# Attention, mixture of experts and a SoLU layer in one launch: row products at full array width, a two-step scale of v, and another order of the attention's steps

## The chip, the cores and the metric

The kernel runs on one NeuronCore of a Trainium2 chip. The engines are named as the profile names them: PE is TensorE (PEld its weight loads), DVE is VectorE, ACT is ScalarE, POOL is GpSimd, and SP is SyncE, which here only issues DMAs. The metric is the device time of one execution in microseconds (us), lower is better. Of the kernel before, three runs took 585.15, 590.14 and 594.05 us, median 590.14 us.

## The reference

Three stages follow one another. First, attention over 2 batches of 8 heads, 768 tokens, head size 64, where a query sees only the keys of its own cluster: each query and key goes to the nearest of 16 centroids, and only pairs with equal clusters count.

```python
q_assign = np.argmax(np.einsum('bhsd,hcd->bhsc', q_n, c_n), axis=-1)
k_assign = np.argmax(np.einsum('bhsd,hcd->bhsc', k_n, c_n), axis=-1)
mask = q_assign[:, :, :, None] == k_assign[:, :, None, :]
scores = scale * np.matmul(q, k.transpose(0, 1, 3, 2))
scores = np.where(mask, scores, -1000000000.0)
scores = scores - np.max(scores, axis=-1, keepdims=True)
attn = np.exp(scores)
attn = attn / (np.sum(attn, axis=-1, keepdims=True) + 1e-09)
return np.matmul(attn, v).astype(np.float32)
```

Its 1536 x 512 result goes through a mixture of 8 experts (each token to the expert of its largest logit: `relu(x @ w1[e]) @ w2[e]`, times two gates), and then through a dense layer: `h = x @ w_in`, SoLU (`h * softmax(h)`), layer norm with a gain, and `@ w_out`. All in single precision.

## The kernel before

The attention takes the 16 heads in eight pairs, `p` = 0 to 7; pairs 0 to 3 are batch 0. A pair's queries and keys stand transposed in one tile `w`, split in a high and a low part, so that products in the fast format keep single precision. Rows 64 to 79 of `w` hold one-hot clusters, which add a huge penalty to a score across clusters. A pair is made of these steps, each a short function that issues a few instructions on several engines:

- `hi`, `lo`, `moves`, `sims`, `red`, `arg0` to `arg2`, `aux0`, `aux1`: split queries and keys, move parts of `w` by DMA, compare with the centroids, take the nearest, and bring the one-hot rows into `w` (by PE, ACT and DMA). For pair 0 `mask` does the last of these straight from PSUM (line 434).
- `x` p.j (j = 0 to 11): one block of 128 queries by all 768 keys on PE (line 485, two matmuls into the one PSUM buffer `pm`), and DVE takes each row's largest (line 487, into column 16 of the tile `ohb` of the pair). The next `x` waits for that reduction, since there is one buffer. `y` does the same in two halves through the two score banks `pS` (lines 498 to 500).
- `row` p.h.half: turns three columns of largest scores into one row. Three matmuls (line 508) have one column of `ohb` as weights and the identity as moving operand, and write PSUM partition 64 (96 in pair 0); ACT negates the row into `w` (line 510).
- `vs0`, `vs1`, `vs2`: a power of two that scales v. DVE takes the largest of v in each partition (line 449); PE turns that column into a row (line 453), DVE takes its largest and makes the power of two on partition 0 (lines 455 to 458); PE sends it to all partitions by a matmul with ones (line 461), DVE copies it out (line 463). `vsp0`, `vsp1` split v by it (ACT line 474, DVE line 476).
- `S` p.u.part: scores of 128 keys by 384 queries (lines 540 and 541) into a bank `pS`, of which there are two, and ACT takes their exponential (line 550). `L` p.u.part: the low part of it, on DVE (`v`) or POOL (`p`), line 558. `A` p.u.part: 18 matmuls of probabilities by v (lines 574 to 576). After a head's last one DVE divides (lines 581 to 584).
- `tr`, `log`, `acc`: a pair's share of the expert logits. `g0.0` (lines 645 to 647), `g0.0.5` and others: place the tokens of batch 0 once pairs 0 to 3 are done. `warmN`: N matmuls on zeros.

Nothing schedules this at run time. Each engine executes its own instructions strictly in the order in which the program issued them, and waits on semaphores. That order is the string `FLAT`, some 800 names of such steps; a loop near the end calls them in turn. A second string, `MOE`, orders the experts' stage in the same manner.

Of the kernel before, what the change touches and what calls it, by code (L numbers as in the profile page):

```python
# [57 lines left out]
S1.4.0 x1.10 lo30p aux21 vs21 S1.4.1 S1.5.0 hi31 L1.1.0p A0.11.1 L1.2.0p x1.11 sims31 red31 tr00 A1.0.0 L1.4.0p S1.5.1
arg30 row111 S1.6.0 vs22 x2.0 S1.6.1 lo31v A1.1.0 tr01 L1.3.0p S1.7.0 S1.7.1 A1.2.0 log0 S1.8.0 arg31 x2.1 acc0 vsp20
A1.3.0 S1.8.1 L1.6.0p S1.9.0 y2.2 x2.3 A1.4.0 L1.8.0p S1.9.1 arg32 L1.5.0p row200 L1.7.0p ld4 S1.10.0 L1.9.0p x2.4  # L60
S1.10.1 aux30 y2.5 A1.5.0 moves3 S1.11.0 x2.6 row201 aux31 S1.11.1 A1.6.0 hi40 S2.0.0 vsp21 sims41 A1.7.0 L1.10.0p
S2.0.1 L1.11.0p late x2.7 zero3 zero4 S2.1.0 vs30 A1.8.0 S2.1.1 x2.8 y2.10 A1.9.0 red41 sims40 ld5 hi41 L2.0.0p x2.9
# [25 lines left out]
S7.5.0 x7.10 row710 A6.10.0 A6.11.0 L7.2.0p L7.3.0v S7.6.0 S7.7.0 x7.11 A7.0.0 A7.1.0 L7.4.0p L7.5.0v tr60 S7.8.0
S7.9.0 tr61 A7.2.0 L7.6.0p L7.7.0v S7.10.0 S7.11.0 log6 row711 A7.3.0 A7.4.0 L7.8.0p L7.9.0v S7.0.1 S7.1.1 acc6 pick0
A7.5.0 A7.6.0 L7.10.0p L7.11.0v pick1 S7.2.1 S7.3.1 pick2 A7.7.0 A7.8.0 L7.0.1p L7.1.1v S7.4.1 S7.5.1 A7.9.0 A7.10.0  # L90
L7.2.1p L7.3.1v S7.6.1 S7.7.1 A7.11.0 A7.0.1 L7.4.1p L7.5.1v w0 S7.8.1 S7.9.1 tr70 A7.1.1 A7.2.1 L7.6.1p L7.7.1v
S7.10.1 S7.11.1 log7 A7.3.1 A7.4.1 L7.8.1p L7.9.1v acc7 g1.0
# [1379 lines left out]
```

## Time and profile before

| | |
|---|---|
| runs | 585.15, 590.14, 594.05 us |
| profiled execution | 591.26 us |
| its span, first to last instruction | 589.5 us |
| mean granted TensorE clock | 0.986 |
| PE busy | 559.0 us, 95% |
| DVE busy | 407.8 us, 69% |
| ACT busy | 295.4 us, 50% |
| POOL busy | 259.0 us, 44% |

The attention lasts until about 256 us of the span, the experts until about 440 us, the dense layer to the end. PE stands beside its time in the whole span, DVE and POOL have most of theirs in the attention. A timeline row gives the start of a merged group in us from the span's start, its length, engine, source line, operation, output and input by the program's names, shapes and count; in brackets is how long the engine sat idle before, and whose end let it go. Lengths of matmuls include their latency, so the pace of PE is read from the starts.

### The profile page before, as it was taken

The page shows a single profiled execution, that of the slowest core. Times are in us where ns is not written, and L with a number is a line of the kernel's source. Part 1 is how long each engine was busy: PE and PEld are TensorE (multiplying, and loading weights), DVE is VectorE, ACT ScalarE, POOL GpSimd, SP SyncE. Part 2 cuts the span into 40 slices and gives each one's busy share as a digit, 9 for nine tenths or more (in the row PEclk, how much of TensorE's full clock was granted, in tenths as well). Part 3 has the DMA queues.
Part 4 walks back from the last instruction along what each step waited for, and adds up shares of the span by engine and source line. Part 5 has one row for each costly group of instructions (what it writes and reads, how often), then busy time and mean ns, then how long its engine had stood idle before and what let it go on. Part 6 is the DMA issues. An engine that isn't in the chain of part 4 may idle for free. (4 is left out here: it accounts for less than half of the span.)

```text
span 589.5 us, 12359 instructions
## 1 busy us (share of the span) xinstructions
PE 559.0 (95%) x4661; PEld 473.4 (80%) x4663; DVE 407.8 (69%) x814; ACT 295.4 (50%) x635; POOL 259.0 (44%) x285
## 2 busy tenths in 40 slices
PE   6999999999989999999999998999999999999995
PEld 2566678777768888898999998989997788888884
DVE  6788987778776889847667588887646845654550
ACT  5765766766745565423222467667655522332230
POOL 7467687888674777530000000320406742333221
PEclk9999999999986999999999999999999999999999
DMA  7258559547231111599939577683300000001000
GB/s 251 82 116 264 138 147 278 148 102 238 62 75 43 34 55 38 188 353 398 378 116 389 198 241 260 217 267 100 100 2 3 0 37 18 19 18 37 18 37 36
DMA packets 28866, 81.06 MB, mean 138 GB/s; under 512 B 5356, under 2 KB 5868, under 8 KB 28804
## 3 DMA queue, kind: packets, MB, share of 16 engines
q1 hardware_dynamic: 26020, 70.80, 37.8%
q0 software_dynamic: 2784, 9.44, 4.4%
q8 instruction: 38, 0.62, 0.4%
q14 instruction: 24, 0.20, 0.1%
HBM read 56.17 MB, written 11.53 MB: 115 GB/s over the span
## 5 line engine op out<-in xcount | busy, mean ns | idle before, releaser
L558 POOL TENSOR_TENSOR pl<-pe 128x768 f16<-128x768 f32 (+1 forms) x99 | 130.6, 1333 | 60.7 <-ACT pe L550 56.5
L550 ACT ACTIVATE pe<-pS 128x384 f32<-128x384 f32 x192 | 88.3, 489 | 68.9 <-PE pS L541 56.7
L487 DVE TENSOR_REDUCE ohb<-pm 128x1 bf16<-128x768 f32 x79 | 75.4, 954 | 31.1 <-PE pm L485 30.6
L540 PE MATMUL pS<-w 81*128 81x384 f32 (+1 forms) x192 | 77.9, 406 | 3.7 <-DVE mh L499 2.4
L541 PE MATMUL pS<-w 128*128 128x384 f32 x192 | 68.1, 355 | 0.0
L574 PE MATMUL pa<-v,pe 128*128 128x65 f16 x576 | 65.1, 197 | 0.0
L574 PEld LDWEIGHTS <-pe 128*128 128x128 bf16 x576 | 53.3, 99 | 14.0 <-issue 11.7
L575 PE MATMUL pa<-v,pe 128*128 128x64 f16 x576 | 64.3, 197 | 0.0
L576 PE MATMUL pa<-v,pl 128*128 128x65 f16 x576 | 64.0, 195 | 0.0
L575 PEld LDWEIGHTS <-pe 128*128 128x128 bf16 x576 | 54.4, 99 | 0.3
L576 PEld LDWEIGHTS <-pl 128*128 128x128 f16 x576 | 54.4, 100 | 0.0
L1034 POOL TENSOR_TENSOR wk<-rw,wk 128x512 fp32r<-128x512 f32 x13 | 18.0, 1395 | 73.9 <-ACT wk L1033 62.0
L485 PE MATMUL pm<-w 80*128 80x512 f32 (+1 forms) x158 | 45.7, 372 | 4.0 <-DVE ohb L487 2.9
L540 PEld LDWEIGHTS pS<-w 81*128 81x128 f32 (+1 forms) x192 | 38.3, 200 | 11.1 <-issue 3.2
L1335 ACT ACTIVATE e<-h,sm,smeta 128x512 f32<-128x512 f32 x24 | 18.5, 774 | 56.7 <-DVE sm L1331 56.7
L1330 DVE TENSOR_REDUCE sm<-h 128x1 f32<-128x512 f32 x24 | 15.4, 685 | 44.5 <-PE h L1041 41.5
L1033 ACT ACTIVATE wk<-rw 128x512 fp32r<-128x512 f32 x62 | 36.6, 631 | 10.4 <-DMA rw<-in_w_dram 8.0
L1034 DVE TENSOR_TENSOR wk<-rw,wk 128x512 fp32r<-128x512 f32 x49 | 34.7, 727 | 8.9 <-ACT wk L1033 8.5
L541 PEld LDWEIGHTS pS<-w 128*128 128x128 f32 x192 | 39.0, 203 | 0.1
L1039 PE MATMUL pf<-m,c 128*128 128x512 f32 x96 | 38.9, 405 | 0.0
L1039 PE MATMUL h<-m,x 128*128 128x512 f32 x96 | 37.7, 393 | 0.4 <-PEq L1295 0.4
L1040 PE MATMUL pf<-m,c 128*128 128x512 f32 x96 | 38.0, 395 | 0.0
(294 smaller groups left out, 1451.1 us busy)
## 6 DMA issues: line engine op xcount, KB each, us to landing
rw<-in_w_dram SPq DMA_DIRECT2D x31, 512.0 KB, 4.4
wk<-in_w_dram SPq DMA_DIRECT2D x25, 512.0 KB, 7.9
w<-w SPq DMA_DIRECT2D x42, 192.0 KB, 3.8
xs_d<-zrow SPq DMA_DIRECT2D x8, 512.0 KB, 5.1
w_w<-in_w_dram SPq DMA_DIRECT2D x8, 512.0 KB, 7.3
raw<-in_qT_dram SPq DMA_DIRECT2D x8, 384.0 KB, 3.7
raw<-in_kT_dram SPq DMA_DIRECT2D x8, 384.0 KB, 4.6
vraw<-in_v_dram SPq DMA_DIRECT2D x8, 384.0 KB, 5.7
```

Source lines behind the costliest of these rows:

```text
L485: nc.tensor.matmul(pm[:, c0:c1], w[0:80, M0 + h, 0, t * 128 : t * 128 + 128], w[0:80, M0 + h, 1, c0:c1], start=True, stop=True)
L487: nc.vector.tensor_reduce(out=s["oh"][:, t, 0, h, C : C + 1], in_=pm, op=ALU.max, axis=AX.X)
L540: nc.tensor.matmul(pS, w[0:kr, M0 + h, 1, ts], w[0:kr, M0 + h, 0, c0:c1], start=b0 == 0, stop=False, skip_group_check=True)
L541: nc.tensor.matmul(pS, w[:, B0 + h, 1, ts], w[:, B0 + h, 0, c0:c1], start=False, stop=True, skip_group_check=True)
L550: nc.scalar.activation(pe[:, e0 - b0 : e0 + n], s["bank"][:, : kb * n], AF.Exp, scale=0.125)
L558: eng.tensor_tensor(out=pl, in0=pe, in1=ph, op=ALU.subtract)
L574: nc.tensor.matmul(pa[:, o0 : o0 + D + 1], ph[:, qs], vh, start=(t == 0 and qt == q0), stop=False, skip_group_check=True)
L575: nc.tensor.matmul(pa[:, o0 : o0 + D], ph[:, qs], vl, start=False, stop=False, skip_group_check=True)
L576: nc.tensor.matmul(pa[:, o0 : o0 + D + 1], pl[:, qs], vh, start=False, stop=(t == NT - 1), skip_group_check=True)
L1034: (eng or nc.vector).tensor_tensor(out=t[:, 1, :], in0=rw, in1=t[:, 0, :].bitcast(F32), op=ALU.subtract)
L1039: nc.tensor.matmul(out, a[0], b[0], start=first, stop=False, skip_group_check=True)
L1040: nc.tensor.matmul(out, a[0], b[1], start=False, stop=False, skip_group_check=True)
```

## The change

Four things, none of which alters what is computed.

1. `row`: the one column of weights is read 65 times (97 in pair 0), so that the product fills PSUM partitions 0 to 64 and not 64 alone. ACT still reads the one row. In `order` this shows as an output of 65x128 where 1x128 stood. The count stays: 96 matmuls.
2. `mask` of pair 0: 80 columns of weights, into partitions 0 to 79, where 16 columns into partitions 64 to 79 stood (24 matmuls). The tile before `ohb0` is 64 columns longer, so that there is something to read.
3. `vs`: the column of largest values is read 128 times as weights against the identity, in single precision, so that every partition has the whole row; DVE reduces and makes the power of two on all 128 partitions. The second matmul, its copy on DVE and one PSUM tile of each pair fall away.
4. `FLAT`: up to `S3.11.0` the string is the old one without `vs02`, `vs12`, `vs22`, `vs32`. From there to the end of the attention, which is from about 136 us of the old span, steps stand in another order. `x5.4` and `x7.2` become `y`, `L4.9.0` and `L5.8.0` go from POOL to DVE, `L6.5.0` from DVE to POOL; in pair 7 four go from POOL to DVE and three from DVE to POOL; `warm1` and `warm4` in pair 4 become `warm1` there and `warm3` in pair 5. `MOE` is unchanged.

```diff
-        w, oh = w_first, ohb[0]
+        w = w_first
         for t in range(n):
-            nc.tensor.matmul(px[t // 3][64:80, t % 3 * 128 : t % 3 * 128 + 128], oh[:, t0 + t, a, h, :C], identb,
+            c0 = ((t0 + t) * 4 + a * 2 + h) * (C + 1)
+            nc.tensor.matmul(px[t // 3][:80, t % 3 * 128 : t % 3 * 128 + 128], first[:, c0 : c0 + 80], identb,
                              start=True, stop=True)
...
-        elif step == 1:
+        else:
             px = ps_x.tile([128, 512], F32, tag="px", name=f"pv_{p}")
-            nc.tensor.transpose(px[0:1, :128], s["am"], identf)
-            m1 = s["m1"] = p2.tile([1, 2], F32, tag="m1", name=f"m1_{p}")
-            nc.vector.tensor_reduce(out=m1[:, 0:1], in_=px[0:1, :128], op=ALU.max, axis=AX.X)
-            nc.vector.tensor_scalar(m1[:, 0:1], m1[:, 0:1], 2.0 ** -100, None, op0=ALU.max)
-            nc.vector.tensor_scalar(bits(m1[:, 0:1]), bits(m1[:, 0:1]), 0x7F800000, None, op0=ALU.bitwise_and)
-            nc.vector.tensor_scalar(bits(m1[:, 1:2]), bits(m1[:, 0:1]), -1.0, float(268 << 23), op0=ALU.mult, op1=ALU.add)
-        else:
-            px = ps_x.tile([128, 512], F32, tag="px", name=f"pvb_{p}")
-            nc.tensor.matmul(px[:, :1], onesf, s["m1"][:, 1:2], start=True, stop=True)
+            nc.tensor.matmul(px[:, :128], s["am"].to_broadcast([128, 128]), identf, start=True, stop=True)
+            m = p2.tile([128, 1], F32, tag="m1", name=f"m1_{p}")
+            nc.vector.tensor_reduce(out=m, in_=px[:, :128], op=ALU.max, axis=AX.X)
+            nc.vector.tensor_scalar(m, m, 2.0 ** -100, None, op0=ALU.max)
+            nc.vector.tensor_scalar(bits(m), bits(m), 0x7F800000, None, op0=ALU.bitwise_and)
             s["vsc"] = p2.tile([128, 1], F32, tag="vsc", bufs=3, name=f"vsc_{p}")
-            nc.vector.tensor_copy(s["vsc"], px[:, :1])
+            nc.vector.tensor_scalar(bits(s["vsc"]), bits(m), -1.0, float(268 << 23), op0=ALU.mult, op1=ALU.add)
...
-            nc.tensor.matmul(px[r, t * 128 : t * 128 + 128], oh[:, half * 3 + t, 0, h, C : C + 1], identb,
-                             start=True, stop=True)
+            nc.tensor.matmul(px[: r.stop, t * 128 : t * 128 + 128],
+                             oh[:, half * 3 + t, 0, h, C : C + 1].to_broadcast([128, r.stop]), identb, start=True, stop=True)
...
-lo70p A4.8.0 L5.0.0p red70 g0.0 sims71 S5.2.0 S5.2.1 x5.11 y6.0 vs61 lo71v A4.9.0 L5.1.0p red71 S5.3.0 S5.3.1 A4.10.0
+L4.11.0p aux61 sims70 S5.0.1 A4.7.0 hi71 x5.9 red70 lo70p S5.1.0 A4.8.0 S5.1.1 x5.10 S5.2.0 sims71 S5.2.1 y6.0 x5.11
```

The moves that matter are on DVE, in pairs 5 and 6. Before, this stood in DVE's queue from the largest of block 10 of pair 5 (`pm_5_10`) to block 0 of pair 6 (`mh_6_0`, a `y`, whose inputs are the two score banks `pS`); `sim_7` is `red70`, and the three rows on `gmx`, `gd` and `ohf` are `g0.0`.

```order
L487 TENSOR_REDUCE ohb5_161<-pm_5_10_3085 128x1
L348 STREAM_TRANSPOSE sim_7_3047<-simc_7_0_3109 128x6x32
L645 TENSOR_REDUCE gmx_128<-lacc0_125 128x6
L646 TENSOR_TENSOR gd_129<-lacc0_125,gmx_128 128x48
L647 SCALAR_TENSOR_TENSOR ohf_127<-gd_129,cst_97 128x48
L487 TENSOR_REDUCE ohb5_161<-pm_5_11_3130 128x1
L499 TENSOR_REDUCE mh_6_0_3134<-pS_161_3135 128x1
L499 TENSOR_REDUCE mh_6_0_3134<-pS_162_3138 128x1
L500 TENSOR_REDUCE ohb6_162<-mh_6_0_3134 128x1
```

In the changed program the same stretch of DVE's queue reads so (the second row is `L4.9.0`, new on DVE; line numbers are two lower there).

```order
L485 TENSOR_REDUCE ohb5_159<-pm_5_8_2990 128x1
L556 TENSOR_TENSOR pl_4_9_0_2888<-pe_4_9_0_2887 128x768
L485 TENSOR_REDUCE ohb5_159<-pm_5_9_3061 128x1
L349 STREAM_TRANSPOSE sim_7_3032<-simc_7_0_3065 128x6x32
L485 TENSOR_REDUCE ohb5_159<-pm_5_10_3097 128x1
L497 TENSOR_REDUCE mh_6_0_3116<-pS_162_3117 128x1
L497 TENSOR_REDUCE mh_6_0_3116<-pS_163_3120 128x1
L498 TENSOR_REDUCE ohb6_160<-mh_6_0_3116 128x1
L485 TENSOR_REDUCE ohb5_159<-pm_5_11_3124 128x1
```

`g0.0` no longer stands ahead of the `y` of pair 6, and that `y` comes ahead of block 11 of pair 5. `g0.0` went to an earlier place in DVE's queue, between blocks 6 and 7 of pair 5, right behind the logits of pair 3 (`acc3`) on which it works:

```order
L485 TENSOR_REDUCE ohb5_159<-pm_5_5_2880 128x1
L620 TENSOR_TENSOR lsum_121<-plg_3_0_2891,lsum_121 128x192
L623 STREAM_TRANSPOSE lacc0_123<-lsum_121 128x192
L485 TENSOR_REDUCE ohb5_159<-pm_5_6_2920 128x1
L643 TENSOR_REDUCE gmx_126<-lacc0_123 128x6
L644 TENSOR_TENSOR gd_127<-lacc0_123,gmx_126 128x48
L645 SCALAR_TENSOR_TENSOR ohf_125<-gd_127,cst_97 128x48
L485 TENSOR_REDUCE ohb5_159<-pm_5_7_2943 128x1
```

Behind it there are now blocks of `x` alone, and no `y`, for four blocks.

## Rows read from the trace of the kernel before

**Rows 1.** Stretches: us; busy us (count) of PE, PEld, DVE, ACT, POOL; clock; DMA.

```profile
100.00:165.00 65.00, 63.06 (x770) 48.38 (x769) 50.28 (x91) 42.41 (x88) 50.63 (x35) 1.00 0.52 140
...
174.00:188.00 14.00, 13.76 (x106) 11.63 (x107) 10.87 (x24) 5.83 (x11) 5.92 (x6) 0.52 0.20 48
...
200.00:256.00 56.00, 53.39 (x778) 46.55 (x774) 49.04 (x121) 27.08 (x63) 37.37 (x46) 1.00 0.31 114
```

**Rows 2.** PE's timeline at a `row` step, and at an `aux` step.

```profile
162.83 0.34 PE L541 MATMUL pS<-w 128*128 128x384 f32 x1
163.10 0.33 PE L508 MATMUL pmr<-identb,ohb 128*1 128x128 bf16 x3
163.36 0.62 PE L485 MATMUL pm<-w 80*128 80x512 f32 x2
...
154.57 0.34 PE L541 MATMUL pS<-w 128*128 128x384 f32 x1
154.74 0.33 PE L406 MATMUL paux<-identb,ohb 128*68 128x128 bf16 x3
154.96 0.62 PE L485 MATMUL pm<-w 80*128 80x512 f32 x2
```

**Rows 3.** Weight loads of these two lines: ns min/median/max, first and last start.

```profile
L508 PEld LDWEIGHTS <-ohb x96: 79/82/126, 15.4 to 234.8; 128*1 128x1 bf16 x96
...
L406 PEld LDWEIGHTS <-ohb x42: 107/111/114, 38.9 to 191.2; 128*68 128x68 bf16 x42
```

**Rows 4.** PE's timeline: the two `vs` matmuls, and single-precision ones at full width.

```profile
150.46 0.19 PE L576 MATMUL pa<-v,pl 128*128 128x65 f16 x1
150.58 0.38 PE L461 MATMUL pvb<-m,onesf 1*128 1x1 f32 x2
150.89 0.62 PE L485 MATMUL pm<-w 80*128 80x512 f32 x2
...
171.35 0.27 PE L453 MATMUL pv<-cst,am 128*1 128x128 f32 x1
171.46 0.19 PE L574 MATMUL pa<-v,pe 128*128 128x65 f16 x1
...
255.07 0.61 PE L896 MATMUL pS<-x2T 128*128 128x128 f32 x4
255.52 0.61 PE L896 MATMUL w_ps<-x2T 128*128 128x128 f32 x4
```

**Rows 5.** PE's timeline at its longest stall, and the same work earlier.

```profile
174.24 0.69 PE L540 MATMUL pS<-w 81*128 81x384 f32 x1 [2.07 <-DVE mh L499]
174.73 0.52 PE L541 MATMUL pS<-w 128*128 128x384 f32 x1
175.05 0.52 PE L540 MATMUL pS<-w 81*128 81x384 f32 x1
...
163.99 0.34 PE L541 MATMUL pS<-w 128*128 128x384 f32 x1
164.16 0.34 PE L540 MATMUL pS<-w 81*128 81x384 f32 x1
```

**Rows 6.** The timelines of DVE and POOL ahead of that stall.

```profile
170.22 1.20 DVE L646 TENSOR_TENSOR gd<-lacc,gmx 128x48 f32<-128x48 f32 x1
171.46 1.39 DVE L647 SCALAR_TENSOR_TENSOR ohf<-gd,cst 128x48 bf16<-128x48 f32 x1
...
173.64 1.01 DVE L499 TENSOR_REDUCE mh<-pS 128x1 f32<-128x384 f32 x2
...
169.90 4.31 POOL L558 TENSOR_TENSOR pl<-pe 128x768 f16<-128x768 f32 x3
```

**Rows 7.** A low part on DVE beside POOL's, and PE behind it: three timelines.

```profile
226.22 3.67 DVE L558 TENSOR_TENSOR pl<-pe 128x384 f16<-128x384 f32 x1
...
225.64 3.82 POOL L558 TENSOR_TENSOR pl<-pe 128x768 f16<-128x768 f32 x4
...
230.81 0.61 PE L485 MATMUL pm<-w 80*128 80x512 f32 x2 [1.01 <-DVE ohb L487]
```

More of the change, by code (lines that the diff above doesn't have):

```diff
@@ L58 @@
[L58 to L62, printed above, removed]
@@ L88 @@
[L88 to L92, printed above, removed]
+vs00 S0.1.0 mask11 mask10 z0.5 x0.4 mask13 S0.2.0 vs01 L0.2.0v L0.0.0p mask12 S0.3.0 row001 l1qp S0.4.0 ld2 L0.1.0v
@@ new lines @@
+sims10 lo10p vsp00 L0.3.0v L0.4.0p S0.5.0 vsp01 S0.0.1 x0.6 S0.1.1 A0.0.0 red10 y0.7 hi11 A0.1.0 sims11 vs10 A0.2.0
+red11 L0.0.1p A0.3.0 x0.8 A0.4.0 L0.1.1p S0.2.1 l1kv arg10 x0.9 arg11 S0.3.1 S0.4.1 row010 lo11p L0.5.0p A0.5.0 S0.5.1
+S0.6.0 arg12 warm1 A0.0.1 A0.1.1 moves1 S0.7.0 hi20 y0.10 L0.6.0p L0.3.1p L0.2.1p aux10 aux11 x0.11 S0.8.0 ld3 sims20
+L0.5.1v S0.9.0 L0.4.1p L0.7.0v A0.2.1 A0.3.1 S0.10.0 S0.11.0 A0.4.1 row011 A0.5.1 A0.6.0 A0.7.0 x1.0 hi21 S0.6.1
+S0.7.1 L0.8.0p vs11 L0.10.0p A0.8.0 x1.1 lo20p S0.8.1 y1.2 x1.3 sims21 L0.11.0p L0.8.1v red21 red20 L0.9.0p A0.9.0
@@ new lines @@
+zero0 zero1 S0.9.1 S0.10.1 A0.10.0 vsp10 x1.4 A0.11.0 L0.9.1p row100 L0.6.1p sims30 x1.5 S0.11.1 L0.7.1p vsp11 A0.6.1
+S1.0.0 row101 y1.6 L0.10.1p arg20 S1.0.1 lo21p L1.0.0p S1.1.0 x1.7 zero2 A0.7.1 L0.11.1p S1.1.1 S1.2.0 A0.8.1 A0.9.1
+x1.8 S1.2.1 arg21 red30 arg22 row110 moves2 hi30 warm2 x1.9 vs20 S1.3.0 A0.10.1 aux20 S1.3.1 S1.4.0 x1.10 lo30p aux21
+vs21 S1.4.1 S1.5.0 hi31 L1.1.0p A0.11.1 L1.2.0p x1.11 sims31 red31 tr00 A1.0.0 L1.4.0p S1.5.1 arg30 row111 S1.6.0 x2.0
+S1.6.1 lo31v A1.1.0 tr01 L1.3.0p S1.7.0 S1.7.1 A1.2.0 log0 S1.8.0 arg31 x2.1 acc0 vsp20 A1.3.0 S1.8.1 L1.6.0p S1.9.0
@@ new lines @@
+y2.2 x2.3 A1.4.0 L1.8.0p S1.9.1 arg32 L1.5.0p row200 L1.7.0p ld4 S1.10.0 L1.9.0p x2.4 S1.10.1 aux30 y2.5 A1.5.0 moves3
+S1.11.0 x2.6 row201 aux31 S1.11.1 A1.6.0 hi40 S2.0.0 vsp21 sims41 A1.7.0 L1.10.0p S2.0.1 L1.11.0p late x2.7 zero3
+zero4 S2.1.0 vs30 A1.8.0 S2.1.1 x2.8 y2.10 A1.9.0 red41 sims40 ld5 hi41 L2.0.0p x2.9 vs31 S2.2.0 S2.2.1 A1.10.0 S2.3.0
+lo40p x2.11 red40 S2.3.1 A1.11.0 row210 S2.4.0 S2.4.1 L2.1.0p L2.2.0p x3.1 S2.5.0 A2.0.0 row211 S2.5.1 S2.6.0 L2.3.0p
+arg40 x3.2 zero5 tr10 arg41 arg42 S2.6.1 S2.7.0 A2.1.0 L2.5.0p A2.2.0 L2.4.0p lo41p A2.3.0 L2.6.0p S2.7.1 tr11 S2.8.0
@@ new lines @@
+x3.3 S2.8.1 A2.4.0 S2.9.0 S2.9.1 x3.0 moves4 ld6 log1 L2.7.0p S2.10.0 aux40 L2.9.0p acc1 vs40 A2.5.0 S2.10.1 S2.11.0
+L2.8.0p row300 aux41 A2.6.0 S2.11.1 S3.0.0 L2.10.0p vsp30 hi50 x3.5 sims51 y3.4 y3.7 x3.6 row301 vsp31 A2.7.0 S3.0.1
+S3.1.0 hi51 lo50p sims50 y3.8 A2.8.0 red50 x3.9 L3.0.0p S3.1.1 S3.2.0 S3.2.1 x3.10 vs41 red51 A2.9.0 S3.3.0 L3.1.0p
+x3.11 S3.3.1 A2.10.0 arg50 L2.11.0p x4.0 S3.4.0 row311 arg51 A2.11.0 S3.4.1 S3.5.0 A3.0.0 lo51p row310 A3.1.0 L3.3.0p
+S3.5.1 x4.1 S3.6.0 L3.2.0p tr20 S3.6.1 x4.2 S3.7.0 arg52 A3.2.0 S3.7.1 tr21 x4.3 L3.5.0p S3.8.0 vsp40 aux50 y4.4
@@ new lines @@
+L3.4.0p x4.5 A3.3.0 S3.8.1 L3.6.0p moves5 S3.9.0 log2 aux51 L3.7.0p L3.8.0p x4.6 S3.9.1 vsp41 S3.10.0 A3.4.0 row401
+x4.7 acc2 S3.10.1 A3.5.0 row400 S3.11.0 A3.6.0 vs50 L3.9.0p zero6 S3.11.1 S4.0.0 y5.0 sims60 hi60 x4.8 S4.0.1 ld7
+S4.1.0 hi61 L3.11.0p L3.10.0p A3.7.0 lo60v x4.10 A3.8.0 S4.1.1 L4.0.0p S4.2.0 zero7 sims61 x4.11 lo61p red61 S4.2.1
+S4.3.0 vs51 A3.9.0 S4.3.1 red60 L4.1.0p x4.9 warm1 row410 A3.10.0 L4.2.0p S4.4.0 S4.4.1 L4.3.0p arg60 x5.1 row411
+L4.4.0p arg61 A3.11.0 S4.5.0 S4.5.1 A4.0.0 x5.2 S4.6.0 arg62 S4.6.1 L4.5.0p A4.1.0 S4.7.0 tr30 moves6 vsp50 S4.7.1
@@ new lines @@
+x5.3 A4.2.0 aux60 row500 y5.4 tr31 vs60 S4.8.0 S4.8.1 vsp51 L4.6.0p A4.3.0 x5.5 S4.9.0 L4.7.0p log3 A4.4.0 acc3 S4.9.1
+x5.6 g0.0 S4.10.0 S4.10.1 S4.11.0 x5.7 L4.8.0p L4.10.0p vs61 row501 A4.5.0 S4.11.1 hi70 x5.8 S5.0.0 L4.9.0v A4.6.0
+L4.11.0p aux61 sims70 S5.0.1 A4.7.0 hi71 x5.9 red70 lo70p S5.1.0 A4.8.0 S5.1.1 x5.10 S5.2.0 sims71 S5.2.1 y6.0 x5.11
+lo71v L5.1.0p A4.9.0 S5.3.0 S5.3.1 red71 L5.2.0p A4.10.0 arg70 row510 S5.4.0 x6.1 warm3 g0.0.5 row511 A4.11.0 S5.4.1
+moves7 L5.3.0p arg71 x6.2 S5.5.0 L5.0.0p S5.5.1 A5.0.0 vsp60 tr40 arg72 S5.6.0 S5.6.1 x6.3 L5.5.0p A5.1.0 vs70 S5.7.0
@@ new lines @@
+S5.7.1 L5.6.0p L5.4.0p x6.4 aux70 tr41 S5.8.0 A5.2.0 x6.5 aux71 log4 vsp61 S5.8.1 L5.7.0p row600 A5.3.0 x6.6 S5.9.0
+S5.9.1 A5.4.0 acc4 L5.8.0v S5.10.0 x6.7 S5.10.1 A5.5.0 S5.11.0 S5.11.1 row601 x6.8 S6.0.0 A5.6.0 L5.10.0p S6.0.1 x6.9
+A5.7.0 L5.11.0p g0.1 S6.1.0 S6.1.1 x6.10 g0.2 A5.8.0 L5.9.0p row610 L6.0.0p S6.2.0 S6.2.1 x6.11 g0.3.5 vs71 S6.3.0
+L6.1.0p A5.9.0 S6.3.1 x7.0 A5.10.0 S6.4.0 L6.2.0v S6.4.1 A5.11.0 S6.5.0 x7.1 g0.3.2 S6.5.1 L6.4.0p L6.3.0p row611 y7.2
+g0.4 A6.0.0 S6.6.0 x7.3 S6.6.1 A6.1.0 tr50 g0.3.3 S6.7.0 S6.7.1 x7.4 A6.2.0 L6.6.0p S6.8.0 L6.5.0p tr51 x7.5 vsp70
@@ new lines @@
+S6.8.1 row700 log5 A6.3.0 S6.9.0 acc5 L6.7.0p S6.9.1 x7.6 A6.4.0 L6.8.0p g0.4.5 row701 S6.10.0 S6.10.1 x7.7 A6.5.0
+L6.9.0v S6.11.0 g0.3.4 A6.6.0 S6.11.1 L6.10.0p g0.3.0 x7.8 S7.0.0 A6.7.0 S7.1.0 A6.8.0 L7.0.0p L6.11.0p vsp71 S7.2.0
+x7.9 S7.3.0 A6.9.0 L7.1.0v S7.4.0 S7.5.0 x7.10 A6.10.0 row710 A6.11.0 L7.2.0p S7.6.0 S7.7.0 L7.3.0v A7.0.0 x7.11
+A7.1.0 L7.4.0p tr60 S7.8.0 g0.3.1 S7.9.0 A7.2.0 L7.8.0p L7.6.0p tr61 S7.10.0 L7.7.0v S7.11.0 L7.5.0v log6 A7.3.0
+A7.4.0 row711 L7.9.0p S7.0.1 S7.1.1 acc6 pick0 A7.5.0 A7.6.0 L7.11.0p L7.10.0p S7.2.1 pick1 S7.3.1 A7.7.0 pick2 A7.8.0
@@ L93 @@
+A7.9.0 S7.4.1 L7.1.1v L7.2.1v L7.0.1v A7.10.0 S7.5.1 A7.11.0 S7.6.1 L7.3.1v L7.5.1v S7.7.1 A7.0.1 S7.8.1 L7.4.1v
+S7.9.1 w0 L7.8.1p tr70 A7.1.1 A7.2.1 S7.10.1 L7.6.1v log7 A7.3.1 S7.11.1 A7.4.1 acc7 L7.9.1v g1.0 L7.7.1p
 """
@@ L275, in body @@
     for j in range(NPR):
-        ohb.append(keep.tile([128, NT, 2, 2, C + 1], BF16, name=f"ohb{j}"))
-    nc.gpsimd.memset(ohb[0], 0.0)
+        if j == 0:
+            first = keep.tile([128, 64 + NT * 4 * (C + 1)], BF16, name="ohb0")
+            ohb.append(first[:, 64:].rearrange("p (t a h c) -> p t a h c", t=NT, a=2, h=2))
+        else:
+            ohb.append(keep.tile([128, NT, 2, 2, C + 1], BF16, name=f"ohb{j}"))
+    nc.gpsimd.memset(first, 0.0)
     nc.gpsimd.memset(w_first[64:96, 1].bitcast(F32), 0.0)
@@ L944, in body @@
             OPS[f"arg{p}{k}"] = lambda p=p, k=k: a_argmax(p, k)
+        for k in range(2):
             OPS[f"vs{p}{k}"] = lambda p=p, k=k: v_scale(p, k)
```

36 lines of the change are left out of this document (1 added, 35 removed).

## The prediction

> **What bounds the kernel now.** I read the stretches first. From 100 to 165 us PE is busy for 63.06 of 65 us, and the next engines, POOL and DVE, for 50.63 and 50.28; from 200 to 256 us it is PE 53.39 of 56 and DVE 49.04 [rows 1]. So PE sets the pace of the attention, with a fifth to an eighth of the time as slack on the others. A microsecond that PE no longer needs there ends the attention nearly a microsecond earlier, and the experts and the dense layer, whose code and order are the same, start that much earlier.
>
> Second, PE's own timeline, for places where it does not run at its pace. There is one that counts. At 172.17 us it stops for 2.07 us, until a DVE reduction lets it go [rows 5], and from then the granted clock is 0.52 over 174 to 188 us, against 1.00 in the stretches I show on either side of it [rows 1]: the 1.2 GHz level for most of it, and then it rose again with PE at work. The idle 1.01 us before 230.81 us was followed by no fall [rows 1, 7].
>
> Third, DVE's timeline for why it came late. `g0.0` stood ahead of the `y` of pair 6. Two of its operations, on 48 columns, took 1.20 and 1.39 us, while POOL ran three low parts without a gap from 169.90 to 174.21 us; so the `y` reductions began at 173.64 us, and the scores behind them needed the banks that these hold [rows 6].
>
> **The sum** goes against the profiled execution, 591.26 us, of which 589.5 us are the span and 1.76 us lie around it. It is 1.12 us above the median of the three runs.
>
> *Row products.* Between a score matmul and the next block there are 0.53 us when a `row` step stands in between (162.83 to 163.36) and 0.39 us for an `aux` step, which also is three 128-column products against the identity but 68 columns wide (154.57 to 154.96) [rows 2]. The gap ahead of it is 0.27 against 0.17 us and behind it 0.26 against 0.22 us, so the narrow step loses its time on entry and exit. The new one is 65 columns wide and I price it as the `aux` step: 0.14 us less. Behind most steps a score or a probability matmul follows, not a block, and there the exit may be worth more: I take 0.18 us over all, between 0, if width is not what costs, and 0.28, twice the difference seen. 32 steps: **-5.8 us**, between 0 and -9.
>
> *v's scale.* The second matmul goes: from the last probability matmul to the next block there are 0.43 us with it in between (150.46 to 150.89), 0.12 of entry and 0.31 of its own [rows 4]; I take 0.40 of them. The first becomes single precision at 128 columns, two instructions at 0.11 us (four in 0.45 us, 255.07 to 255.52), where it was one of 0.11 us (171.35 to 171.46) plus an entry like a row step's, 0.10 more than an `aux` step's [rows 2, 4]: +0.01. Eight pairs: **-3.1 us**, between -2 and -4. DVE loses a copy per pair and reduces as many elements in a row as before; that is off the path, as POOL's slightly larger fill is at the start. What is late next there is `vsp`, which only needs the scale earlier.
>
> *Masks of pair 0.* 24 narrow products in four steps, of which the first two wait for the clusters and are waited for by ACT. I price each as a row step, 0.14 us [rows 2], and count three: **-0.4 us**, between 0 and -1.
>
> *The stall and the clock.* In the new order no `g0.0` stands ahead of that `y`, only block 10's reduction and no low part. So the 2.07 us should go. A mean of 0.52 over 14 us is 13.4 us at the lower level; there score matmuls start 0.32 us apart and at the upper level 0.17 us apart [rows 5]. By that ratio the work takes 7.1 us, by the ratio of the clocks 6.7 us, but matmuls that wait for a load or an engine do not shrink: I take 7.5 us. **-2.1 - 5.9 = -8.0 us**, between 0, if a new stall takes its place (below), and -8.8.
>
> *What takes some back.* Two more blocks become `y`, which hold both score banks for two reductions of 0.5 us each (1.01 for two) [rows 6]: 0.4 us each, **+0.8**, between 0 and 2. `g0.0` still has to pass DVE, now ahead of block 7 of pair 5; if POOL is as busy there, block 7's reduction is 2.6 us late and block 8 waits for it, with four score steps, a probability step and a row step to cover it: **+0.5**, between 0 and 2.1 (the old stall again). `L4.9.0` and `L5.8.0` on DVE lie between two blocks of `x`; their cover is the slack of the one `pm` buffer, **+0.5**, between 0 and 2 x 1.01 [rows 7]. And with 9.3 us less on PE the other engines, already at 77 to 88% [rows 1], will be the late ones more often: a fifth of it, **+1.9**, between 0 and 9.3. `aux` of pair 6 stands later, close ahead of the `y` that needs its DMAs; I count 0. The SP queue keeps its sequence.
>
> Sum: -5.8 - 3.1 - 0.4 - 8.0 + 0.8 + 0.5 + 0.5 + 1.9 = -13.6, so 591.3 - 13.6 = 577.7, **578 us**.
>
> **A rule that speaks against it.** The weight loads of 68 columns take 111 ns against 82 ns for one column [rows 3], yet the wide step as a whole is the shorter one [rows 2], so the load is hidden. The Trainium skill, TensorE: Matmul & The Clock Gate, section LDWEIGHTS (loading the stationary operand), gives a load's time as its number of columns over 1.2 GHz; by that a product of 65 columns would need 54 ns of loading (an estimate from that page) and one of a single column next to none, and if loads were exposed the sum would be the worse by 96 x 54 ns = 5.2 us. By the rows that would be 96 x 29 ns = 2.8 us at most, and it is a rival below.
>
> **The rivals.**
>
> *A new stall takes the old one's place* (25%). DVE waits for POOL in many places: a low part of 384 columns took 3.67 us because POOL ran four of its own from 225.64 to 229.46 us, and ended 0.43 us behind the last of them [rows 7]. Any of the three steps newly on or moved on DVE can meet that. It decides when PE is stopped for as long as 2.07 us, behind which the clock fell; behind 1.01 us it did not. Price: 2.1 us and 5.9 us again, 578 + 8 = 586 us. For it: the order is new from 136 us on, and the old one had such a stall in those 120 us. Against: behind `g0.0` there are now blocks of `x` alone, which leave the score banks free.
>
> *Both new places stall, and the clock falls twice* (7%): this ends on the other side. The mechanism is POOL's run of low parts holding a DVE operation past several of them, at `g0.0` and at a low part. From two falls on: 578 + 2 x 8.0 = 594 us, 0.5% above the median before. For it speaks that DVE did not get in between POOL's operations there [rows 7]. The Trainium skill, SBUF: State Buffer, section Who interferes with whom, has whoever issues first hold the shared ports for one instruction and the other wait. By that rule DVE would wait for one of POOL's operations, of 1.4 us (4.31 for three [rows 6]), not for four, no such place would stop PE for 2 us, and this rival would fall away; the row says otherwise, so it keeps its chance.
>
> *PE is no longer the engine that is waited for* (12%). The 9.3 us of work taken off PE come back as waits on DVE and POOL, and only the stall and the clock are gained: 591.3 - 8.0 + 1.8 = 585 us. Against it: PE's slack is 3 to 5%, theirs 12 to 22% [rows 1].
>
> *The row products gain nothing* (6%), since the exposed loads eat what entry and exit gave: 578 + 5.8 = 584 us; then the change does not do what it says in its largest plain term.
>
> *More than the sum* (4%): the cover holds everywhere and the four additions are nil, 578 - 3.7 = 574 us, and with the row products at their bound of 0.28 us each 571 us.
>
> **The numbers.** The forecast of 578 us has 46%, with its own spread of 573 to 582 us. The range should leave out two in ten: 571 to 589 us holds all but the double fall and the tails. A measurement of this kernel can tell about 2%, 11.8 us, from no change; 2% under the median is 578.3 us, just at the forecast, so its chance splits: a good half of it (27%) and the better case (4%), with the lower tail of the row and cover cases (5%), make faster 0.36. Slower by 2% would be over 602 us, three falls or a fault that I do not see: 0.04. Within 2%: 0.60.
>
> **What would show it.** Right: the `row` step between a score matmul and a block at 0.39 us and no longer 0.53; no second matmul for v and the first at 0.22 us; no stall of PE of 2 us between 30 and 256 us and a granted clock of 1.00 there; the attention's end some 13 to 14 us earlier, and an unchanged distance from there to the end. Wrong: a clock under 0.9 in any stretch after 30 us; PE's waits for `ohb` and `mh` grown by several us; or a longer time from the attention's end to the end.

## The result, and the profile after

| | before | changed |
|---|---|---|
| median of the first measurement | 589.51 us (4 runs) | 580.44 us (4 runs, 577.35 to 582.53) |
| ratio, 95% interval | | 0.9845, 0.9803 to 0.9888 |
| the same two kernels once more | 590.49 us (17 runs) | 582.61 us (6 runs), ratio 0.9865, 0.982 to 0.991 |
| profiled execution | 591.26 us, span 589.5 | 579.94 us, span 578.1 |
| mean granted clock in it | 0.986 | 0.996 |

The change is worth 8 to 9 us, 1.35 to 1.55%: a real gain, though under 2%. The forecast was 578 us. The time is near it, but the way there was not the one that I summed.

PE's timeline in the changed kernel shows the two edited steps; first a `row` step between a score matmul and a block, then the first (now only) matmul of v's scale, and last a score matmul with a probability matmul right behind it.

```profile
186.56 0.33 PE L539 MATMUL pS<-w 128*128 128x384 f32 x1
186.73 0.33 PE L506 MATMUL pmr<-identb,ohb 128*65 128x128 bf16 x3
186.87 0.60 PE L483 MATMUL pm<-w 80*128 80x512 f32 x2
...
140.98 0.33 PE L539 MATMUL pS<-w 128*128 128x384 f32 x1
141.16 0.38 PE L455 MATMUL pv<-cst,am 128*128 128x128 f32 x2
141.38 0.19 PE L572 MATMUL pa<-v,pe 128*128 128x65 f16 x1
...
213.99 0.34 PE L539 MATMUL pS<-w 128*128 128x384 f32 x1
214.17 0.20 PE L572 MATMUL pa<-v,pe 128*128 128x65 f16 x1
```

From score to block there are 0.31 us (186.56 to 186.87), where [rows 2] had 0.53: the entry fell from 0.27 to 0.17, the exit from 0.26 to 0.14. The second matmul of v's scale is gone. The remaining one, two instructions, adds 0.40 - 0.18 = 0.22 us between score and probability matmul, as I had priced it. The `row` step came out shorter than the 0.39 us of the `aux` step that I took for it.

The stall of [rows 5] is gone. The stretches (us; busy us and count of PE, PEld, DVE, ACT, POOL; clock; DMA) show it, and what came instead:

```profile
100.00:165.00 65.00, 62.99 (x824) 50.48 (x821) 54.40 (x101) 44.81 (x92) 53.26 (x37) 1.00 0.51 137
174.00:188.00 14.00, 13.54 (x186) 11.49 (x186) 12.06 (x20) 10.02 (x21) 7.60 (x6) 1.00 0.22 48
...
218.00:222.00 4.00, 4.00 (x54) 3.69 (x51) 2.40 (x5) 1.33 (x3) 0.65 (x1) 0.57 0.17 66
```

At 174 to 188 us the clock is 1.00, where [rows 1] had 0.52. But at 218 to 222 us it is 0.57, most of that stretch at the 1.2 GHz level. Ahead of it PE, DVE and POOL did this (timeline; in brackets the idle time before, and whose end let it go):

```profile
217.39 0.61 PE L483 MATMUL pm<-w 80*128 80x512 f32 x2 [1.71 <-DVE ohb L485]
...
212.50 3.96 DVE L474 SCALAR_TENSOR_TENSOR v<-vraw,vsc,v 128x768 f16<-128x768 f32 x1
216.39 0.95 DVE L485 TENSOR_REDUCE ohb<-pm 128x1 bf16<-128x768 f32 x1
...
210.96 1.62 POOL L701 DMA_INDIRECT xs_d<-x2T,posi  x1 [0.16 <-issue]
212.61 3.03 POOL L556 TENSOR_TENSOR pl<-pe 128x384 f16<-128x384 f32 x3
```

POOL issues an indirect DMA (`g0.3.0`) until 212.58 us. Then it runs three low parts without a gap, and DVE's `vsp71`, which takes 1.01 us at the median of its eight, takes 3.96. It ends 0.8 us behind POOL's third. The reduction of the block comes behind it, and PE stops for 1.71 us. This is what [rows 7] shows, at a new place. There too POOL had issued an indirect DMA right ahead of its run of low parts, which began at 225.64 us:

```profile
224.16 1.46 POOL L703 DMA_INDIRECT xs_d<-x2T,posi  x1 [0.21 <-issue]
```

The way from the attention's end to the end changed too. The first matmuls of the experts and of the dense layer, in the kernel before and in the changed one:

```profile
256.66 0.60 PE L1118 MATMUL ph<-x2T,w_w 128*128 128x128 f32 x3 [0.54 <-ACT x2T L1003]
...
437.89 0.39 PE L1039 MATMUL h<-m,x 128*128 128x512 f32 x1
```

```profile
247.85 0.38 PE L1117 MATMUL ph<-x2T,w_w 128*128 128x128 f32 x1 [0.53 <-ACT x2T L1002]
...
426.63 0.39 PE L1038 MATMUL h<-m,x 128*128 128x512 f32 x1
```

The attention ends 8.81 us earlier, not 13 to 14. The experts take 178.78 us, where they took 181.23: 2.45 us less, with code and order untouched. The dense layer is the same within 0.1 us. In the experts' stage the table of PE's waits (us, times, longest) has this line before, and these two after:

```profile
PE pt L1086 <- DMA xs<-xs_d: 4.1, 5, 1.9
```

```profile
PE pt L1085 <- DMA xs<-xs_d: 1.0, 1, 1.0
PE po L1119 <- DVE h L1153: 0.7, 1, 0.7
```

So most of the 2.45 us are waits for gathered rows: these are 3.1 us less, and PE's other waits there, mainly the second line, 0.9 us more. Whether the change shortened them or the execution did is taken up below. A second profile of the changed kernel divides the gain otherwise: its attention ends 6.8 us earlier than before (at 249.86 us), and its experts take 176.84 us.

### The profile page after: what moved, and what is told of

Read it like the earlier page. It is cut to its first block, busy times and chain, and to the rows that moved or that the text cites. A ratio compares the mean times of both kernels' runs of the same rounds, so it can differ in the third digit from the quotient of the medians.

```text
span 578.1 us, 12327 instructions
## 1 busy us (share of the span) xinstructions
PE 547.7 (95%) x4652; PEld 469.4 (81%) x4654; DVE 403.9 (70%) x811; ACT 296.5 (51%) x635; POOL 256.9 (44%) x283
## 5 line engine op out<-in xcount | busy, mean ns | idle before, releaser
L556 POOL TENSOR_TENSOR pl<-pe 128x768 f16<-128x768 f32 (+1 forms) x97 | 128.8, 1347 | 54.6 <-ACT pe L548 48.3
L485 DVE TENSOR_REDUCE ohb<-pm 128x1 bf16<-128x768 f32 x77 | 73.4, 954 | 23.6 <-PE pm L483 23.3
L572 PEld LDWEIGHTS <-pe 128*128 128x128 bf16 x576 | 52.9, 98 | 13.9 <-issue 13.4
L483 PE MATMUL pm<-w 80*128 80x512 f32 (+1 forms) x154 | 43.8, 366 | 5.6 <-DVE ohb L485 3.2
L1033 DVE TENSOR_TENSOR wk<-rw,wk 128x512 fp32r<-128x512 f32 x49 | 36.4, 761 | 7.4 <-ACT wk L1032 7.1
```

The source lines that it names most:

```text
L483: nc.tensor.matmul(pm[:, c0:c1], w[0:80, M0 + h, 0, t * 128 : t * 128 + 128], w[0:80, M0 + h, 1, c0:c1], start=True, stop=True)
L485: nc.vector.tensor_reduce(out=s["oh"][:, t, 0, h, C : C + 1], in_=pm, op=ALU.max, axis=AX.X)
L556: eng.tensor_tensor(out=pl, in0=pe, in1=ph, op=ALU.subtract)
L572: nc.tensor.matmul(pa[:, o0 : o0 + D + 1], ph[:, qs], vh, start=(t == 0 and qt == q0), stop=False, skip_group_check=True)
L1033: (eng or nc.vector).tensor_tensor(out=t[:, 1, :], in0=rw, in1=t[:, 0, :].bitcast(F32), op=ALU.subtract)
```

## The experiments

All medians stand beside runs of the kernel before on the same chip: 589.75 us (32 runs) for the first four, 590.49 us (17) for the next four, 590.45 us (11) for the last four. The ratio is to these runs, and gains in us are worked out from it. It is not the quotient of the two medians; where the medians say much less, that is given too.

### The three edits in the old order

```diff
 up to S3.11.0: the old string without vs02 to vs42, as in the changed kernel
-behind S3.11.0: the new order of steps
+behind S3.11.0: the old order of steps, without vs52, vs62, vs72
```

> The three code edits (wide row products, two-step scale of v, wide masks) with the old order of steps, the third step of v's scale left out of it. Theory A, the forecast's terms: 9.3 us less work on PE, a fifth of it lost to late engines, so 7.4 us less, 582 us; the stall of 2.07 us ahead of the y of pair 6 and the fall of the clock behind it are still there. Theory B, the spared time comes back as waits on DVE and POOL, as pairs 0 to 4 of the changed kernel hint (3.3 us gained up to the first score of pair 5, where these terms come to 6): 4 us less at most, 585 to 587 us. Theory C, the stall hangs on the exact timing and goes here too: 574 to 576 us.

588.28 us, ratio 0.9963 (0.9937 to 0.999): 2 us (1.5 by the medians). Theory A and C fall, and B was still too hopeful. How so is shown by two rows, from the first matmul of an `aux` step, by which the kernels have issued the same steps, to the last score: of the kernel before and of this one.

```profile
39.07:243.51 204.44, 196.20 (x2462) 156.88 (x2462) 165.25 (x307) 127.15 (x273) 150.48 (x120) 0.97 0.43 120
```

```profile
37.78:240.87 203.09, 189.28 (x2457) 156.21 (x2456) 165.02 (x300) 127.05 (x273) 151.20 (x120) 0.97 0.44 121
```

PE's busy time is 6.9 us less (196.20 to 189.28), at a mean clock of 0.97 in both. But the stretch is only 1.4 us shorter: PE idles 13.8 us (203.09 - 189.28), where it idled 8.2. Its waits in this kernel, from 31 us on:

```profile
PE pm L483 <- DVE ohb L485: 5.2, 5, 1.7
PE pS L538 <- DVE mh L497: 2.3, 2, 1.9
PE pm L483 <- DMA w<-aux: 2.1, 2, 1.1
PE pm L483 <- DVE top L393: 1.7, 1, 1.7
```

The old stall is there (1.9, for `mh`), and so are three for DVE of up to 1.7 us. A PE with less to do reaches the same late DVE earlier.

### The row products alone, in the old order

```diff
-nc.tensor.matmul(px[r, ...], oh[:, half * 3 + t, 0, h, C : C + 1], identb, ...)
+nc.tensor.matmul(px[: r.stop, ...], oh[..., C : C + 1].to_broadcast([128, r.stop]), identb, ...)
```

> The kernel before with the wide row products alone. Theory A: 32 steps of 0.18 us, 5.8 us less on PE, 4.6 to 5.8 us less in time, 584 to 585 us, with the stall and the fall of the clock in place. Theory B, waits take back half: 587 us. Rival that the products gain nothing since the wide loads are exposed: 589 to 590 us, and the row step between a score matmul and a block at 0.53 us as before.

586.91 us, ratio 0.9951 (0.9916 to 0.9986): 2.9 us, as theory B has it. The products do gain; the rival with exposed loads falls.

### The scale of v alone, in the old order

```diff
-step 1: transpose, power of two on partition 0; step 2: matmul with ones, copy
+step 1: one matmul against identf, power of two on all partitions
```

> The kernel before with the two-step scale of v alone. Theory A: 8 matmuls and their entry fewer, 3.1 us less, 586 us. Theory B: the new first matmul, single precision and 128 columns wide, is dearer on PE by about 0.1 us than I priced and waits take back some: 1 to 2 us less, 587.5 to 588.5 us.

589.1 us, ratio 0.9976 (0.9947 to 1.0005): 1.4 us (0.7 by the medians), as theory B has it, and not told apart from nothing.

### g0.0 moved, old code and old order

```diff
-lo70p A4.8.0 L5.0.0p red70 g0.0 sims71
+lo70p A4.8.0 L5.0.0p red70 sims71
-A4.4.0 x5.6 S4.10.0
+A4.4.0 x5.6 g0.0 S4.10.0
```

> The kernel before with one move: g0.0 (three DVE operations and what they feed) stands between x5.6 and S4.10.0 and no longer ahead of the y of pair 6. Theory A: the stall of 2.07 us and the 14 us at the lower clock go, 8 us less, 581 to 582 us, granted clock 0.996 over all. Rival: POOL's run of low parts holds another DVE operation there and the stall only moves: 588 to 590 us, clock 0.986. Rival 2: the stall goes, but PE is then held at g0.0's new place: a stall near 157 us and the same time as before.

588.5 us, ratio 0.9956 (0.9927 to 0.9985): 2.6 us (1.3 by the medians), not 8. Its stretch and PE's longest wait there:

```profile
174.00:188.00 14.00, 12.18 (x157) 9.74 (x157) 12.03 (x26) 7.72 (x17) 10.53 (x9) 1.00 0.42 100
```

```profile
180.90 0.61 PE L485 MATMUL pm<-w 80*128 80x512 f32 x2 [1.34 <-DVE ohb L487]
```

The 2.07 us and the low clock are gone, as theory A had it. Yet DVE, busy all but 0.23 us from 174.87 us on with the two `y` reductions, v's scale, a low part of a key and a comparison with centroids, comes late to the next block of `x` too. In the kernel before that wait was covered by the stall and the low clock ahead of it.

### The new order alone, old code

```diff
 up to S3.11.0: the old string with vs02 to vs42
-behind S3.11.0: the old order of steps
+behind S3.11.0: the new order of steps, with vs52, vs62, vs72 kept
```

> The kernel before with the new order of steps and none of the three code edits; the third step of v's scale stands in it as in the old string up to S3.11.0 and then some 10 to 15 steps behind the second. With the old order the three edits together gave 1.5 us and PE waited that much more. Theory B, the order makes the gain and the edits little by themselves: 582 to 584 us. Theory A, the forecast's terms: the order gives its 8.0 us less the 1.8 that it costs, 583.5 us, and the edits the rest. Theory D, order and edits need each other (the order was fitted to the lighter PE): 586 us or more, with new stalls of PE of over 1.5 us.

585.89 us, ratio 0.9924 (0.9897 to 0.9951): 4.5 us, between theory A and D. Of its stalls over 1.5 us ahead of the last score there is one, that for `vsp71`; the two of pair 5 are both gone. The wait and the stretch around it:

```profile
224.03 0.62 PE L485 MATMUL pm<-w 80*128 80x512 f32 x2 [1.71 <-DVE ohb L487]
```

```profile
218.00:232.00 14.00, 12.29 (x187) 9.95 (x186) 11.74 (x17) 7.11 (x17) 9.44 (x11) 1.00 0.11 40
```

It is as long as in the changed kernel, and here the clock did not fall behind it.

### g0.0 put back, in the changed kernel

```diff
-x5.6 g0.0 S4.10.0
+x5.6 S4.10.0
-x5.10 S5.2.0 sims71
+x5.10 g0.0 S5.2.0 sims71
```

> The changed kernel with one move undone: g0.0 stands ahead of the y of pair 6 again, behind x5.10. Theory A: the stall of about 2 us near 166 us comes back, and in many executions a fall of the clock behind it: 583 to 585 us. Rival: without the run of low parts that POOL had there in the old order, or with block 11 behind the y, the three DVE operations cost PE nothing: 580 to 581 us.

582.98 us, ratio 0.9879 (0.9833 to 0.9926), 0.4 us above the changed kernel beside it and no stall at that place: the rival was right. The timelines of DVE and POOL:

```profile
167.65 0.70 DVE L644 TENSOR_TENSOR gd<-lacc,gmx 128x48 f32<-128x48 f32 x1
168.39 0.21 DVE L645 SCALAR_TENSOR_TENSOR ohf<-gd,cst 128x48 bf16<-128x48 f32 x1
...
166.82 1.47 POOL L556 TENSOR_TENSOR pl<-pe 128x768 f16<-128x768 f32 x1 [0.31 <-ACT pe L548]
168.55 1.47 POOL L556 TENSOR_TENSOR pl<-pe 128x768 f16<-128x768 f32 x1 [0.26 <-ACT pe L548]
```

The same two operations that took 1.20 and 1.39 us in [rows 6] take 0.70 and 0.21, since POOL runs one low part, idles 0.26 us, and runs the next, where it ran three in a row before. So `g0.0`'s place by itself makes no stall; in the old order it took POOL's run beside it, and moving `g0.0` away from that run (above) took the stall away as well. Whether it helps too that block 11 now stands behind the `y`, no experiment tells.

### The scatter behind pair 7's run of low parts

```diff
-L6.10.0p g0.3.0 x7.8
+L6.10.0p x7.8
-S7.8.0 g0.3.1 S7.9.0
+S7.8.0 g0.3.1 g0.3.0 S7.9.0
```

> The changed kernel with one move: g0.3.0, an indirect DMA that POOL issues at 210.96 us for 1.62 us, stands behind g0.3.1, where POOL has 5 us to spare. In the changed kernel its low parts pile up behind it, POOL runs three of them without a gap from 212.61 to 215.64 us, DVE's vsp71 takes 3.96 us where its median is 1.01, and PE stops for 1.71 us. Theory E, the backlog holds DVE: vsp71 at 1 to 2 us, no PE stall over 1 us there, 2 to 3.5 us less, 577 to 578.5 us. Rival: the low parts merely run back to back a little earlier, another DVE operation is held for 3 us and the time stays at 580 us.

580.13 us, ratio 0.9833 (0.9781 to 0.9884). A second measurement:

> The changed kernel with g0.3.0 behind g0.3.1 once more: 578 to 580.5 us, 2 to 3 us less than the changed kernel, vsp71 at 1 us and no stall of PE near 215 us; the last score near 232 us.

580.22 us, ratio 0.9834 (0.9801 to 0.9867). From the second profile, DVE and POOL at that place, and the stretch up to the last score:

```profile
212.16 1.50 DVE L474 SCALAR_TENSOR_TENSOR v<-vraw,vsc,v 128x768 f16<-128x768 f32 x1
213.66 0.96 DVE L485 TENSOR_REDUCE ohb<-pm 128x1 bf16<-128x768 f32 x1
...
212.01 4.86 POOL L556 TENSOR_TENSOR pl<-pe 128x384 f16<-128x384 f32 x4 [1.59 <-ACT pe L548]
```

```profile
31.00:231.00 200.00, 190.19 (x2509) 154.24 (x2508) 165.87 (x319) 131.33 (x280) 150.37 (x120) 1.00 0.48 131
```

Theory E holds at that place: `vsp71` takes 1.50 us, as in all three profiles with the scatter late, where the six with the new order and the scatter ahead have 3.96 or 3.97. PE has no stall there, the clock is 1.00 all the way, and the last score starts at 231.61 us, 3.2 us earlier than in the changed kernel (234.83). The 577 to 578.5 us of the theory were not reached, since of these 3.2 us the whole kernel shows less: 580.2 us is the median of the 12 runs and 581.5 us that of the 10 of the changed kernel (580.13 and 582.61 us on the one chip that ran both), which their spread of 577 to 585 us does not tell apart. In the first of the two profiles the clock fell behind the attention's end instead (0.51 over 247.5 to 251 us).

### The changed kernel again

> The changed kernel once more, beside the others on the same chip: 580 us, 577 to 583 in single executions; a stall of PE near 215 us behind vsp71 if it belongs to the order, and a fall of the clock behind it in some executions and not in others.

582.61 us; the stall behind `vsp71` is there again (3.97 us, last score at 235.18 us).

### The row products narrow again, in the new order

```diff
-nc.tensor.matmul(px[: r.stop, ...], oh[..., C : C + 1].to_broadcast([128, r.stop]), identb, ...)
+nc.tensor.matmul(px[r, ...], oh[:, half * 3 + t, 0, h, C : C + 1], identb, ...)
```

> The changed kernel with the row products narrow again (one column of weights, one partition out), the rest unchanged. Theory A, the forecast's term: PE has 5.8 us more to do and the time is 4.6 to 5.8 us longer than the changed kernel's, 586 to 587 us where that has 581. Theory B, two fifths of what PE is spared come back as its waits in this order: 3 to 3.5 us longer, 584 to 585 us, PE's busy time from 31 us to the last score some 6 us longer and its waits 2 to 3 us shorter. Rival: it gives nothing, 581 us.

585.68 us, ratio 0.99 (0.9861 to 0.994), 2 to 3 us above the changed kernel by the ratios, whose intervals overlap: nearest to theory B. The two rows, of this kernel and of the changed one, from the first `aux` matmul to the last score:

```profile
39.63:239.46 199.83, 192.14 (x2471) 150.97 (x2471) 161.29 (x307) 128.27 (x274) 147.41 (x118) 0.99 0.45 126
```

```profile
38.67:234.83 196.16, 186.95 (x2471) 152.11 (x2471) 161.40 (x307) 128.33 (x274) 148.41 (x118) 0.99 0.46 129
```

PE's busy time is 5.2 us shorter with the wide products, 0.18 us for each of the 29 steps in this stretch, and its idle time 1.5 us longer (7.69 to 9.21).

### Two blocks later

```diff
-A0.7.0 x1.0 hi21 S0.6.1 S0.7.1 L0.8.0p
+A0.7.0 hi21 S0.6.1 S0.7.1 x1.0 L0.8.0p
-S1.6.0 x2.0 S1.6.1 lo31v A1.1.0 tr01
+S1.6.0 S1.6.1 lo31v A1.1.0 x2.0 tr01
```

> The changed kernel with three moves: g0.3.0 behind g0.3.1, as in the run with the late scatter, and the blocks x1.0 and x2.0, which wait 1.2 to 1.4 us for the DMAs that bring the rows of aux, two steps later each (x1.0 behind S0.7.1, x2.0 behind A1.1.0). Theory F, such a wait costs what it lasts: 1.3 to 1.8 us less than the late scatter alone, 577.5 to 579 us where that has 580. Rival: the wait is only moved to the reduction of the next block, the same time.

This kernel has the late scatter too. 582.2 us, ratio 0.9844 (0.9811 to 0.9877): no gain over the late scatter. The two waits are gone but for 0.4 us, yet the profile has a new one of their kind in pair 4, with the clock at 0.83 in the stretch around it:

```profile
122.55 0.59 PE L483 MATMUL pm<-w 80*128 80x512 f32 x2 [2.40 <-DMA w<-aux]
```

```profile
118.00:128.00 10.00, 7.59 (x105) 6.72 (x102) 6.61 (x15) 3.47 (x8) 6.50 (x5) 0.83 0.69 155
```

The profile of the changed kernel has no such wait in pair 4. The DMAs of `aux` land 2.2 us after issue at the median and up to 6.8 us in this execution, 4.6 in that one. The wait does not need the move: the profile of the next experiment, whose order up to there is that of the changed kernel, has the same wait.

```profile
119.09 0.59 PE L483 MATMUL pm<-w 80*128 80x512 f32 x2 [2.33 <-DMA w<-aux]
```

In the profile of the kernel with the two blocks later the clock also fell at the place of the first moved block, where PE's waits were of 0.4 to 0.6 us:

```profile
46.00:56.00 10.00, 8.96 (x73) 6.08 (x72) 7.20 (x17) 3.51 (x7) 4.62 (x8) 0.66 0.83 284
```

So that execution does not show what the two waits cost, and theory F stays open.

### x for the two new y

```diff
-x5.3 A4.2.0 aux60 row500 y5.4
+x5.3 A4.2.0 aux60 row500 x5.4
-row611 y7.2 g0.4
+row611 x7.2 g0.4
```

> The changed kernel with its two new y blocks (5.4 and 7.2) as x blocks through the one buffer pm again. The forecast priced the two at 0.8 us of extra time, so by that 580.2 us where the changed kernel has 581. Rival: the y took waits on pm away, and without them there are two new waits of 0.5 to 1 us: 581.5 to 583 us.

585.06 us, ratio 0.9884 (0.9847 to 0.9921). That the `y` cost 0.8 us is not borne out: without them the kernel is 1 to 2 us slower, though the intervals overlap. That they gain is not shown either, since this profile has the wait of 2.33 us in pair 4, ahead of both blocks. PE waits 5.3 us for reductions of `pm`, against 3.2 in the changed kernel:

```profile
PE pm L483 <- DVE ohb L485: 5.3, 7, 1.8
```

## Why the prediction was right, and where its sum was not

**What bounds the kernel.** Right: PE sets the pace, and what the edits take off it was sized well. Row products: 5.2 us of PE's busy time in 29 of the 32 steps, 0.18 us a step, as forecast. All three edits: 7.0 us in the new order, by these rows of the new order alone and of the changed kernel's second profile, each from the first `aux` matmul to the last score and with one short fall of the clock (7.1 us by the first profile). The terms of the 29 row steps and seven pairs in it come to 5.2 + 2.7 = 7.9, so the scale of v, left with some 1.9 us where it had 2.7, was priced somewhat high.

```profile
38.93:240.34 201.41, 194.09 (x2477) 152.11 (x2478) 161.93 (x314) 128.47 (x274) 147.03 (x118) 0.99 0.44 124
```

```profile
37.88:235.18 197.30, 187.07 (x2471) 152.21 (x2471) 161.47 (x307) 128.19 (x274) 148.45 (x118) 0.99 0.46 128
```

**What takes some back.** Too small. I let a fifth, 1.9 us, come back as waits. In these two rows PE's idle time goes from 7.3 to 10.2 us: 2.9 us, two fifths (1.9 us, a quarter, by the first profile). In the old order it was 5.6 of 6.9. That is the rival in which PE is no longer the engine waited for, in part: by the ratios the edits gave 2 us in the old order and 3.5 to 4.7 in the new one (0.9924 against 0.9865 and 0.9845), where the forecast had 7.4.

**The stall and the clock.** This is the step that failed: the mechanism was right, the size of 8.0 us was not. `g0.0`'s move alone gave 2.6 us. Two things were wrong with the size. The stall covered a second wait some 6 us behind it, which then showed (1.34 us). And the 14 us at the lower clock belonged to the one profiled execution, as three other kernels with this stall suggest. That with the wide row products alone has the same stall, and far less of the lower clock behind it:

```profile
173.73 0.44 PE L540 MATMUL pS<-w 81*128 81x384 f32 x1 [2.07 <-DVE mh L499]
```

```profile
174.00:188.00 14.00, 13.54 (x158) 11.44 (x157) 10.84 (x25) 9.04 (x19) 8.49 (x7) 0.88 0.19 45
```

A mean of 0.88 is 3.4 us at the lower level; the three edits in the old order and the scale of v alone, with stalls of 1.94 and 1.95 us there, have 0.88 too. At the forecast's rate (5.9 us for 13.4) that is 1.5 us, an estimate, so the term comes to 2.1 + 1.5 - 1.3 = 2.3 us, near the 2.6. Even against the profiled execution it was too large: from the 121st to the 169th exponential of the scores, the same work, that took 57.1 us (166.29 to 223.37) and the kernel with `g0.0` moved 51.9 (169.49 to 221.36). The runs say the same: of the 32 runs of the kernel before, the 9 with a mean clock of 0.995 or more have a median of 587.7 us and the 15 under 0.988 one of 591.3. So a run with hardly any fall is about 2 us under the median (589.75). I had summed from 591.26 us.

**A new stall.** That rival came true, POOL's run of low parts holding a DVE operation over several of them and PE behind a block, at a price of about 3 us instead of 8: 1.71 us and a short fall. With it came one of the signs of being wrong, a clock under 0.9. I had searched the three steps newly on or moved on DVE; it hit `vsp71`, which stood ahead of `g0.3.0` and the next two low parts in the old string and behind them in the new one, in a stretch of the diff that I had not walked through. And I had taken the runs of [rows 6] and [rows 7] for one thing. In [rows 6] each operation of `g0.0` was held for one low part only (POOL's three end near 171.3, 172.8 and 174.2 us, the two operations at 171.42 and 172.85), and two such waits in a row were enough to stop PE for 2.07 us; so "no such place would stop PE for 2 us" does not follow. In [rows 7] one operation was held over four, behind an indirect DMA of POOL (more below). The double fall at 594 us would have been 0.7% above the median of 590.14, not 0.5.

**What I priced as a cost.** For the two `y` no cost was found, and the new place of `g0.0` made no difference (0.4 us). The low parts on DVE and the masks of pair 0 were not tried apart.

**Why 578 was near.** Partly by luck. From the median of 590 us the sum would have been 590.1 - 13.6 = 576.5. The true gain of 8 to 9 us is three fifths to two thirds of 13.6; the base, 1.1 us above the median, and a range that reached over the rival's case held the time. The first measurement lay besides below the second, 580.44 against 582.61 us.

**The unpredicted 2.45 us in the experts' stage** are not settled. The five profiles with the old order have 179.1 to 181.2 us there, eight of the nine with the new order 176.8 to 178.8, and the ninth, the first of the late scatter, 181.9. That points to the order, with about 2 us of the gain. But the waits for gathered rows differ from execution to execution, and so few profiles don't part the order from chance.

## What to carry to other kernels

Price a stall from several executions, not from the one that was profiled: the granted clock of every run says how much of it the median has. Look behind a stall that you remove for the wait that it covers. And look at what POOL does right behind an indirect DMA: here the DVE operation that met its run there paid for two to four of POOL's operations, and for one beside its other runs.
